# Attention, dense FFN and routed experts on one core: in the opening, key and query evictions split between ScalarE and VectorE, tile scores ordered ahead of weight work, and the global value rows copied on the chip

## The chip, the core and the metric

The kernel runs on one core of a Trainium2 chip. TensorE (PE) does matmuls and transposes, VectorE (DVE), ScalarE (ACT) and GpSimd (POOL) work elementwise, SyncE (SP) here only issues DMAs. Each engine takes its own instructions strictly in the order in which they were written, and a semaphore holds an instruction back until its inputs are there. The metric is the device time of one execution in microseconds (us), lower is better.

## What is computed

Local and global attention for 4 batches, 8 heads, 512 local and 32 global positions, head width 64; its output goes through a dense FFN, and that through a routed FFN with 8 experts. Cut to what matters here:

```python
s_ll = scale * q_l @ k_l.T            # only keys within 32 positions; the rest is masked
s_lg = scale * q_l @ k_g.T
a_l  = softmax(concat([s_lg, s_ll]))  # per row: minus the maximum, exp, divided by the sum
out_l = a_l @ concat([v_g, v_l])
x = relu(x @ w_in) ** 2 @ w_out       # 512 -> 2048 -> 512, weights given as 64-bit floats
x = x + gate * (relu(x @ w1[e]) @ w2[e])   # rows with skip score > 0, one of 8 experts each
```

## The kernel before

**Tiles.** A tile is 128 query positions; two tiles are a block, 4 tiles a batch. Names carry the tile: `sc2_0` and `sc2_1` are the two halves (even and odd heads) of the scores of tile 2, `sm` the masked scores, `mx` their row maxima, `pT` the transposed probabilities, `po` the product with the values, `xt` its division by the row sums, `xtr` the transposed result, which ACT copies into `x0` for tiles 0 and 1. A tile goes through `attention(t)` in six steps: the scores of both halves with mask, maximum and exp of half 0; the same for half 1; two transposes of the probabilities with an eviction each; values and division; transpose of the result.

**Keys and queries of batch 0.** Heads lie apart in memory, so `load_k` and `load_q` bring them in as they lie and a copy (`puts`, tokens P00, P01, P0, P1) puts them into the order that the transposes want. `prep_k(b, p)` transposes one of four head pairs into PSUM and evicts it to `kT`; `prep_q(j)` does two pairs with two evictions each into `qT`. Their PSUM tiles (`ktr`, `qtr`, and also `sc*_1`, `ptr`, `xtr`) share two places, taken in turn, so every transpose waits for the eviction of the one before the last.

**Values.** A tile reads up to four windows of 96 local value rows, with the 32 global rows below them in partitions 96 to 127. `load_v` brings each window by one DMA and the global rows by another (192 KB and 64 KB); for tiles 0 and 1 into seven opening places, later into six rotating ones (`vr`), which get their global rows once per batch.

**Weights.** The dense weights come as 64-bit floats in 32 chunks of 128x512: for each quarter of the FFN four chunks `in_k` and four chunks `out_f`. Each chunk is rebuilt as a 32-bit float by ACT (L219, `rebase`) and three DVE instructions (L223, L227, L233). Token A does one step of that: L219 for chunk i+1, then L227 of i, L223 of i+1, L233 of i. L227 of a chunk waits for its L219. Block 0 uses the chunks of the first three quarters as they are, in 4-pass float matmuls.

**Dense FFN of block 0.** For f = 0 to 15: `first(f)` (four matmuls into `h`, relu on ACT into `g`), square (`gh`, on ACT after token E, on DVE after F), and one step later `second(f)` (four matmuls into `acc`).

**What sets the order.** SEQ is a list of tokens written out by hand: W fetches a weight chunk, A is the step above, V loads half of a tile's windows, `0a` is the next step of tile 0 of block 0, `0b` of tile 1, `1a`, `1b` of tiles 2 and 3, F0, E0, I0, H0 move the FFN of block 0. Every token writes its instructions to all engines at once, so a token's place in SEQ is its place on each engine. The line that the change of evictions rests on is, in `prep_k`:

```python
nc.scalar.copy(kT[b][:, p, 0:SL].rearrange("p (q j) -> p j q", j=TPB), tr)
```

Of the kernel before, what the change touches and what calls it, by code (L numbers as in the profile page):

```python
# [18 lines left out]


SEQ = """
    Lk01 Lk00 P00 Lg0 0G P01 Lq0 P0 00 02 V Lq1 01 0q W 03 W A W W 0a A V V 0a A W W A 0a 0b 0a 0b A 0b W P1 W 0a A
    0b A V 0a W 0b V A 1q W W A 0b V 1a W W F0 A W E0 1a W W A W V 1a A F0 W 1a I0 A 1b L9 1a H0 V A A W V E0 W 1a
    X0 H0 A A E0 H0 W H0 A H0 W 1b E0 Lg1 A A W W A E0 1b W H0 A 1b E0 A H0 A E0 Lv00 A W W W 1g A I0 C 1b A 1g I0 W
    A D H0 Lv01 1g W E0 A E0 A I0 1g W C C 1g C W E0 A 1g Lq2 C Lk10 A H0 1g I0 2q A C C F0 2G Lk11 E0 I0 20 C E0 21
    22 F0 1b F1 23 C D F0 H1 C C V R00 2a F1 D H1 E1 2a E1 D R00 2a H1 R00 R01 C H1 C C F1 I1 R01 V 2b R01 E1 D A F1
# [28 lines left out]
def attention_ffn_routed_experts(  # L55
# [22 lines left out]
    nc = tc.nc  # L78
    B, H, SL, D = q_l.shape
    SG = q_g.shape[2]  # L80
    P = 128
# [8 lines left out]
    TPB = SL // P  # L90
# [3 lines left out]
    WIN = 3 * SEG  # L94
# [176 lines left out]
    kT, kin, qT, qin, qgT, vgr = {}, {}, {}, {}, {}, {}  # L271
    xts, whole = {}, []
    puts = {}

    def heads(t):
        return t.rearrange("p (h d) -> p h d", h=H)
# [5 lines left out]
    def load_k(b, z):  # L282

        kin[b, z] = stage(f"k{b}_{z}").rearrange("p (j h d) -> p j h d", h=4, j=TPB)
        if b == 0:
            t = stage(f"k{b}_{z}_in").rearrange("p (h j d) -> p h j d", h=4, j=TPB)
            nc.sync.dma_start(t, k_l[b, 4 * z:4 * z + 4].rearrange("h (p j) d -> p h j d", j=TPB))  # L290
            puts[f"{b}{z}"] = lambda: nc.scalar.copy(kin[b, z], t.rearrange("p h j d -> p j h d"))
            return
        for h in range(4):
            nc.sync.dma_start(kin[b, z][:, :, h, :], k_l[b, 4 * z + h].rearrange("(p j) d -> p j d", j=TPB))
# [31 lines left out]
    def prep_k(b, p):  # L326
        tr = pair(f"ktr{b}_{p}")
        for j in range(TPB):
            two = kin[b, p // 2][:, j, 2 * (p % 2):2 * (p % 2) + 2, :]
            nc.tensor.transpose(tr[:, j, :], two.rearrange("p r d -> p (r d)"), ident)  # L330
        nc.scalar.copy(kT[b][:, p, 0:SL].rearrange("p (q j) -> p j q", j=TPB), tr)

    def prep_q(j):
        qT[j] = sb("qT", 1, [P, NPAIR, BLK], f"qT{j}")
        for z in range(2):
            tr = pair(f"qtr{j}_{z}").rearrange("p (a i) q -> p a i q", a=2)
            for a in range(2):
                for i in range(2):
                    h = 2 * (2 * z + a)
                    two = qin[j][:, i, h:h + 2, :]  # L340
                    nc.tensor.transpose(tr[:, a, i, :], two.rearrange("p r d -> p (r d)"), ident)
            for a in range(2):
                nc.scalar.copy(qT[j][:, 2 * z + a, :].rearrange("p (q i) -> p i q", i=2), tr[:, a])

    def window(tt, i):
        return min(max(tt * P + i * SEG - SEG, 0), SL - WIN)
# [6 lines left out]
    def load_v(t, part):  # L353
# [3 lines left out]
        for i in range(2 * part, 2 * part + 2):  # L357
# [4 lines left out]
            if t < 2:  # L362

                k, half = divmod(len(opening), 2)
                if half == 0:
                    opening_places.append(stage(f"v{k}"))
                w = opening_places[k][:, half * DM:(half + 1) * DM]
                opening.append(w)
                nc.sync.dma_start(heads(w[0:WIN]), v_l[b, :, w0:w0 + WIN, :].rearrange("h s d -> s h d"))
                nc.sync.dma_start(heads(w[WIN:P]), v_g[b].rearrange("h s d -> s h d"))  # L370
                vin[t, i] = w
                continue
            k = loaded[0] % 6
# [3 lines left out]
            nc.sync.dma_start(heads(windows[k][0:WIN]), v_l[b, :, w0:w0 + WIN, :].rearrange("h s d -> s h d"))  # L377
            if globals_in.get(k) != b:
                globals_in[k] = b
                nc.sync.dma_start(heads(windows[k][WIN:P]), v_g[b].rearrange("h s d -> s h d"))  # L380
            assert all(w is not windows[k] for w in vin.values())
            vin[t, i] = windows[k]

# [1195 lines left out]
```

## Time and profile before

| | |
|---|---|
| time, median of 3 runs | 712.71 us (711.06 to 715.13) |
| profiled execution | 706.99 us, span of the core 705.3 us |
| mean granted TensorE clock | 0.985 |
| busy in the span | PE 97%, DVE 56%, ACT 52%, POOL 23% |
| TensorE busy from 0 to 45 us | 31.8 us of 45 |
| DMA from 0 to 60 us | 16.18 MB, mean 270 GB/s |

Shares are means over the whole program. In the stretch that the change touches, roughly the first 50 us, they are others: TensorE has gaps and a granted clock of 0.5 to 1, and VectorE is the fullest engine. A granted clock of 1 is 2.4 GHz, 0.5 is 1.2 GHz.

### The profile page before, as it was taken

How to read it: one execution, taken by the hardware profiler on the slowest of the kernel's cores; microseconds unless marked ns; L12 is line 12 of the kernel's file. 1: busy time of each engine (PE TensorE's matmuls, PEld its weight loads, DVE VectorE, ACT ScalarE, POOL GpSimd, SP SyncE). 2: the span in 40 equal slices, each digit the busy share in tenths (PEclk: the TensorE clock that was granted, in tenths of full speed). 3: DMA queues.
4: the chain of work that ended last, by engine and by line, in shares of the span. 5: the costliest groups of instructions: out<-in, count | busy, mean ns of one | idle time of the engine just before them, and what ended most of it. 6: DMA issues, size and time to landing. Idle time of an engine off the chain costs nothing. (4 is left out here: it accounts for less than half of the span.)

```text
span 705.3 us, 18628 instructions
## 1 busy us (share of the span) xinstructions
PE 680.9 (97%) x7621; PEld 573.8 (81%) x7621; DVE 395.0 (56%) x1072; ACT 365.2 (52%) x939; POOL 163.9 (23%) x206
## 2 busy tenths in 40 slices
PE   6689998999999999999999999999999999999996
PEld 4566667889888988888888998888887887898875
DVE  1889964872655165275426526544238733915985
ACT  5767568675535555453465445344434514614863
POOL 6000053453212212211211221122220432401311
PEclk8799999999999999999999999999999999999998
DMA  9999643064063401306340120410026689952930
GB/s 276 247 303 288 235 117 80 2 161 96 2 147 90 111 32 36 84 2 147 99 102 32 45 67 2 162 62 1 32 87 194 213 268 346 372 218 82 359 123 22
DMA packets 118841, 94.20 MB, mean 134 GB/s; under 512 B 84805, under 2 KB 91973, under 8 KB 118740
## 3 DMA queue, kind: packets, MB, share of 16 engines
q1 hardware_dynamic: 108352, 71.01, 35.9%
q10 hardware_dynamic: 8292, 15.48, 6.8%
q0 software_dynamic: 2096, 6.36, 2.7%
q8 instruction: 64, 1.05, 0.6%
q14 instruction: 37, 0.30, 0.2%
HBM read 80.57 MB, written 12.66 MB: 132 GB/s over the span
## 5 line engine op out<-in xcount | busy, mean ns | idle before, releaser
L184 POOL TENSOR_TENSOR gl<-g,gh 128x256 fp32r<-128x256 f32 x107 | 79.5, 743 | 302.8 <-ACT gh L183 142.3
L700 PE MATMUL h<-xh,w_in 128*128 128x256 f32 x464 | 135.1, 291 | 0.7 <-ACT xh L183 0.7
L701 PE MATMUL h<-xl,w_in 128*128 128x256 f32 x464 | 129.7, 280 | 0.3 <-DVE xl L184 0.3
L702 PE MATMUL h<-xh,w_in 128*128 128x256 f32 x464 | 129.8, 280 | 0.0
L725 PE MATMUL acc<-w_out,gh 128*128 128x512 f32 x232 | 97.6, 421 | 1.5 <-ACT gh L183 1.5
L727 PE MATMUL acc<-w_out,gl 128*128 128x512 f32 x232 | 91.9, 396 | 0.2
L726 PE MATMUL acc<-w_out,gh 128*128 128x512 f32 x232 | 91.7, 395 | 0.0
L700 PEld LDWEIGHTS h<-xh,w_in 128*128 128x128 f32 x464 | 87.2, 188 | 4.2 <-ACT xh L183 0.9
L701 PEld LDWEIGHTS h<-xl,w_in 128*128 128x128 f32 x464 | 87.3, 188 | 2.6 <-DVE xl L184 0.5
L704 ACT ACTIVATE g<-h 128x256 f32<-128x256 f32 x128 | 48.7, 381 | 77.0 <-PE h L702 43.7
L702 PEld LDWEIGHTS h<-xh,w_in 128*128 128x128 f32 x464 | 87.2, 188 | 0.0
L433 ACT ACTIVATE sm<-sm,mx 128x128 f32<-128x128 f32 x120 | 46.7, 390 | 49.5 <-DVE mx L431 49.5
L741 DVE TENSOR_TENSOR g<-h,g 128x256 f32<-128x256 f32 x53 | 22.2, 419 | 85.5 <-ACT g L704 85.5
L183 ACT CAST gh<-g 128x256 fp32r<-128x256 f32 x116 | 47.1, 406 | 42.2 <-DVE g L741 40.1
L727 PEld LDWEIGHTS acc<-w_out,gl 128*128 128x128 f32 x232 | 43.6, 188 | 11.9 <-POOL gl L184 1.3
L725 PEld LDWEIGHTS acc<-w_out,gh 128*128 128x128 f32 x232 | 43.6, 188 | 8.5 <-ACT gh L183 1.9
L726 PEld LDWEIGHTS acc<-w_out,gh 128*128 128x128 f32 x232 | 43.8, 189 | 5.7
L426 DVE TENSOR_TENSOR sm<-sc,mask 128x512 f32<-128x512 f32 x30 | 20.6, 687 | 23.3 <-PE sc L413 22.6
L255 POOL TENSOR_TENSOR w_in<-st_raw_in,w_in 128x512 fp32r<-128x512 f32 x10 | 13.0, 1308 | 80.0 <-ACT w_in L251 80.0
L743 ACT ACTIVATE g<-g 128x256 f32<-128x256 f32 x63 | 26.3, 417 | 5.0 <-ACT g L704 2.5
L413 PEld LDWEIGHTS sc<-kT,qT 64*32 64x32 f32 x2048 | 25.2, 110 | 4.3 <-issue 3.5
L413 PE MATMUL sc<-kT,qT 64*32 64x32 f32 (+1 forms) x2048 | 27.4, 230 | 0.0
(718 smaller groups left out, 1461.9 us busy)
## 6 DMA issues: line engine op xcount, KB each, us to landing
st_e<-in_moe_w_dram SPq DMA_DIRECT2D x46, 512.0 KB, 7.5
vr<-in_v_l_dram SPq DMA_DIRECT2D x49, 192.0 KB, 4.3
st_raw_in<-in_moe_w_in_dram SPq DMA_DIRECT2D x16, 512.0 KB, 6.6
st_raw_out<-in_moe_w_out_dram SPq DMA_DIRECT2D x16, 512.0 KB, 8.2
st_e<-in_moe_w_dram ACTq DMA_DIRECT2D x12, 512.0 KB, 5.5
x2d<-x ACTq DMA_DIRECT2D x19, 256.5 KB, 3.7
st_gv<-in_v_l_dram SPq DMA_DIRECT2D x8, 512.0 KB, 4.5
out_dram<-x ACTq DMA_DIRECT2D x16, 256.0 KB, 3.5
```

The source lines that it names most:

```text
L183: nc.scalar.copy(hi, src)
L184: (lo_engine or nc.vector).tensor_tensor(out=lo, in0=src, in1=hi.bitcast(F32), op=ALU.subtract)
L413: nc.tensor.matmul(scs[g][SEG * i:SEG * (i + 1), p, cols], lhsT=q[rows, p, SEG * i:SEG * (i + 1)], rhs=kT[b][rows, p, keys], start=True, s ...
L433: nc.scalar.activation(sm[:, hh, :], sm[:, hh, :], AF.Exp, bias=mx[:, hh:hh + 1], scale=SCALE, accum_out=osum[:, 2 * hh + g:2 * hh + g + 1],)
L700: nc.tensor.matmul(h, lhsT=wh, rhs=xh[:, k, :], start=(k == 0), stop=False)
L701: nc.tensor.matmul(h, lhsT=wh, rhs=xl[:, k, :], start=False, stop=False)
L702: nc.tensor.matmul(h, lhsT=wl, rhs=xh[:, k, :], start=False, stop=(k == KD - 1))
L704: nc.scalar.activation(g, h, AF.Relu)
L725: nc.tensor.matmul(acc[z], lhsT=gh[:, c], rhs=wh, start=first_one, stop=False)
L726: nc.tensor.matmul(acc[z], lhsT=gh[:, c], rhs=wl, start=False, stop=False)
L727: nc.tensor.matmul(acc[z], lhsT=gl[:, c], rhs=wh, start=False, stop=last_one)
L743: nc.scalar.activation(square, g, AF.Square)
```

## The change

Three things, all in the opening.

1. Of the copies and evictions that ACT did for keys and queries, DVE takes the reordering copy of the second half of the keys (P01), the evictions of head pairs 2 and 3 in `prep_k`, and of the second pairs of the first query block in `prep_q`.
2. The first part of SEQ is rewritten. The two halves of a tile's scores follow each other (`0a 0a`, `0b 0b`) with the A tokens behind them, the first two weight chunks are fetched ahead of the values, the second block's queries are loaded later, and F0 stands ahead of `1a`. From token X0 on nothing differs; the set of instructions up to there is the same but for points 1 and 3.
3. The global value rows of batch 0 come by one DMA; POOL copies them from there to the other six opening places and to the six rotating ones. SP issues 12 DMAs of 64 KB less, and POOL runs 12 copies of 32x512 more.

```diff
@@ SEQ
-    Lk01 Lk00 P00 Lg0 0G P01 Lq0 P0 00 02 V Lq1 01 0q W 03 W A W W 0a A V V 0a A W W A 0a 0b 0a 0b A 0b W P1 W 0a A
-    0b A V 0a W 0b V A 1q W W A 0b V 1a W W F0 A W E0 1a W W A W V 1a A F0 W 1a I0 A 1b L9 1a H0 V A A W V E0 W 1a
+    Lk01 Lk00 P00 Lg0 0G P01 Lq0 P0 00 02 W W V 01 0q W W 03 A 0a V 0a A Lq1 0a 0a A V W 0b 0b V 0a W A W P1 0a 0b
+    0b W A W V 0b 0b W V 1q W F0 A 1a W A E0 A 1a A W V F0 A 1a W W I0 A 1a A 1b W W W L9 1a H0 V A A A W V E0 W 1a
@@ load_k
-            puts[f"{b}{z}"] = lambda: nc.scalar.copy(kin[b, z], t.rearrange("p h j d -> p j h d"))
+            copy = nc.vector.tensor_copy if z else nc.scalar.copy
+            puts[f"{b}{z}"] = lambda: copy(kin[b, z], t.rearrange("p h j d -> p j h d"))
@@ prep_k
-        nc.scalar.copy(kT[b][:, p, 0:SL].rearrange("p (q j) -> p j q", j=TPB), tr)
+        copy = nc.vector.tensor_copy if b == 0 and p > 1 else nc.scalar.copy
+        copy(kT[b][:, p, 0:SL].rearrange("p (q j) -> p j q", j=TPB), tr)
@@ prep_q
-                nc.scalar.copy(qT[j][:, 2 * z + a, :].rearrange("p (q i) -> p i q", i=2), tr[:, a])
+                copy = nc.vector.tensor_copy if j == 0 and z else nc.scalar.copy
+                copy(qT[j][:, 2 * z + a, :].rearrange("p (q i) -> p i q", i=2), tr[:, a])
@@ load_v, the seven opening places
+                if len(opening) == 1:
+                    nc.sync.dma_start(heads(w[WIN:P]), v_g[b].rearrange("h s d -> s h d"))
+                else:
+                    nc.gpsimd.tensor_copy(w[WIN:P], opening[0][WIN:P])
                 nc.sync.dma_start(heads(w[0:WIN]), v_l[b, :, w0:w0 + WIN, :].rearrange("h s d -> s h d"))
-                nc.sync.dma_start(heads(w[WIN:P]), v_g[b].rearrange("h s d -> s h d"))
@@ load_v, the six rotating places
-                nc.sync.dma_start(heads(windows[k][WIN:P]), v_g[b].rearrange("h s d -> s h d"))
+                if b == 0:
+                    nc.gpsimd.tensor_copy(windows[k][WIN:P], opening[-1][WIN:P])
+                else:
+                    nc.sync.dma_start(heads(windows[k][WIN:P]), v_g[b].rearrange("h s d -> s h d"))
```

VectorE ahead of tile 0's scores and in them, before (a chunk's three instructions are those on `st_raw`):

```order
L310 COPY st_q0_213<-st_q0_in_214 128x1024
L223 TENSOR_SCALAR st_raw_in_0_0_256<-st_raw_in_0_0_256 128x512
L426 TENSOR_TENSOR sm0_0_339<-sc0_0_273,mask0_75 128x512
L430 TENSOR_REDUCE mx0_0_341<-sm0_0_339 128x4
L431 TENSOR_SCALAR mx0_0_341<-mx0_0_341 128x4
L227 SCALAR_TENSOR_TENSOR st_raw_in_0_0_256<-st_raw_in_0_0_256 128x512
L223 TENSOR_SCALAR st_raw_in_1_0_264<-st_raw_in_1_0_264 128x512
L233 SCALAR_TENSOR_TENSOR st_raw_in_0_0_256<-st_raw_in_0_0_256 128x512
L426 TENSOR_TENSOR sm0_1_362<-sc0_1_274,mask0_75 128x512
```

The same place after:

```order
L292 COPY st_k0_1_188<-st_k0_1_in_189 128x1024
L311 COPY st_q0_213<-st_q0_in_214 128x1024
L333 COPY kT0_198<-ktr0_2_223 128x4x128
L346 COPY qT0_242<-qtr0_1_250 128x2x128 x2
L333 COPY kT0_198<-ktr0_3_261 128x4x128
L223 TENSOR_SCALAR st_raw_in_0_0_229<-st_raw_in_0_0_229 128x512
L435 TENSOR_TENSOR sm0_0_336<-sc0_0_270,mask0_75 128x512
L439 TENSOR_REDUCE mx0_0_338<-sm0_0_336 128x4
L440 TENSOR_SCALAR mx0_0_338<-mx0_0_338 128x4
L435 TENSOR_TENSOR sm0_1_350<-sc0_1_271,mask0_75 128x512
```

One key copy, two key evictions and two query evictions have come to DVE, that of `ktr0_2` behind the query copy, and the second half of the scores follows the first at once; between tile 1's halves no chunk stood before or stands now.

VectorE from the division of tile 1 (`xt1`) to the scores of tile 2, before:

```order
L461 TENSOR_TENSOR xt1_598<-po1_563,osum1_390 128x512
L227 SCALAR_TENSOR_TENSOR st_raw_out_2_492<-st_raw_out_2_492 128x512
L223 TENSOR_SCALAR st_raw_out_3_495<-st_raw_out_3_495 128x512
L233 SCALAR_TENSOR_TENSOR st_raw_out_2_492<-st_raw_out_2_492 128x512
L227 SCALAR_TENSOR_TENSOR st_raw_out_3_495<-st_raw_out_3_495 128x512
L223 TENSOR_SCALAR st_raw_in_0_1_561<-st_raw_in_0_1_561 128x512
L233 SCALAR_TENSOR_TENSOR st_raw_out_3_495<-st_raw_out_3_495 128x512
L426 TENSOR_TENSOR sm2_0_714<-sc2_0_648,mask1_101 128x512
```

and after:

```order
L470 TENSOR_TENSOR xt1_596<-po1_561,osum1_391 128x512
L227 SCALAR_TENSOR_TENSOR st_raw_out_0_389<-st_raw_out_0_389 128x512
L223 TENSOR_SCALAR st_raw_out_1_517<-st_raw_out_1_517 128x512
L233 SCALAR_TENSOR_TENSOR st_raw_out_0_389<-st_raw_out_0_389 128x512
L435 TENSOR_TENSOR sm2_0_709<-sc2_0_643,mask1_101 128x512
L439 TENSOR_REDUCE mx2_0_711<-sm2_0_709 128x4
L440 TENSOR_SCALAR mx2_0_711<-mx2_0_711 128x4
```

At `xt1` the chunk in hand is `out_0` where it was `out_2`, and one step of weight work stands between `xt1` and tile 2's scores where there were two. On TensorE, behind the transposes of the second query block, the four matmuls of `h0_0` now stand ahead of the 128 of `sc2`; before, `sc2` came first.

ScalarE from the result of tile 1 to the eviction of tile 2's transposed probabilities, before (L704 is the relu, L743 the square of an FFN step):

```order
L468 COPY st_x0_559<-xtr1_633 128x4x128
L433 ACTIVATE sm2_0_714,osum2_647<-sm2_0_714,mx2_0_716 128x128 x4
L704 ACTIVATE g0_0_732<-h0_0_727 128x256
L219 ACTIVATE st_raw_in_1_1_625<-st_raw_in_1_1_625 128x512
L743 ACTIVATE gh0_0_740<-g0_0_732 128x256
L704 ACTIVATE g0_1_747<-h0_1_742 128x256
L433 ACTIVATE sm2_1_749,osum2_647<-sm2_1_749,mx2_1_751 128x128 x4
L219 ACTIVATE st_raw_in_2_1_627<-st_raw_in_2_1_627 128x512
L444 COPY pT2_0_779<-ptr2_0_774 128x512
```

and after:

```order
L477 COPY st_x0_531<-xtr1_598 128x4x128
L346 COPY qT1_614<-qtr1_0_615 128x2x128 x2
L346 COPY qT1_614<-qtr1_1_622 128x2x128 x2
L713 ACTIVATE g0_0_636<-h0_0_631 128x256
L219 ACTIVATE st_raw_out_1_517<-st_raw_out_1_517 128x512
L442 ACTIVATE sm2_0_709,osum2_642<-sm2_0_709,mx2_0_711 128x128 x4
L219 ACTIVATE st_raw_out_2_523<-st_raw_out_2_523 128x512
L752 ACTIVATE gh0_0_724<-g0_0_636 128x256
L713 ACTIVATE g0_1_731<-h0_1_726 128x256
L219 ACTIVATE st_raw_out_3_547<-st_raw_out_3_547 128x512
L442 ACTIVATE sm2_1_737,osum2_642<-sm2_1_737,mx2_1_739 128x128 x4
```

The relu of the first FFN step has moved ahead of tile 2's exps, its square still stands behind them and behind one more weight step; two weight steps follow the second half's exps before `pT2_0`, where one did.

## Rows read from the trace of the kernel before

**Rows 1.** The page: busy us, share of the span, instructions.
```profile
PE 680.9 (97%) x7621; PEld 573.8 (81%) x7621; DVE 395.0 (56%) x1072; ACT 365.2 (52%) x939; POOL 163.9 (23%) x206
```
**Rows 2.** Windows: stretch, length, busy PE, PEld, DVE, ACT, POOL; granted clock, DMA, GB/s.
```profile
16.57:69.85 53.28, 44.66 (x716) 32.52 (x717) 48.14 (x97) 36.36 (x113) 0.00 (x0) 0.90 1.05 277
```
**Rows 3.** Timeline, 0 to 45 us and DVE at 82: start, length; keys and queries.
```profile
8.05 1.06 ACT L291 COPY st_k<-st_k_in 128x1024 f32<-128x1024 f32 x1
9.26 0.69 DVE L310 COPY st_q<-st_q_in 128x1024 f32<-128x1024 f32 x1 [7.87 <-DMA st_q_in<-in_q_l_dram]
...
10.31 2.08 ACT L331 COPY kT<-ktr 128x512 f32<-128x512 f32 x2 [0.20 <-PE ktr L330]
...
11.44 2.12 PE L341 MATMUL qtr<-ident,st_q 128*128 128x128 f32 x8 [0.16 <-ACT kT L331]
...
14.36 2.04 PE L413 MATMUL sc<-kT,qT 64*32 64x96 f32 x128
...
82.20 0.67 DVE L507 COPY gpT<-gptr 128x512 f32<-128x512 f32 x1
```
**Rows 4.** Timeline, 0 to 45 us: scores, exps, weight steps and division, tiles 0, 1.
```profile
16.57 0.69 DVE L426 TENSOR_TENSOR sm<-sc,mask 128x512 f32<-128x512 f32 x1 [2.73 <-PE sc L413]
...
18.09 0.68 DVE L227 SCALAR_TENSOR_TENSOR st_raw_in<-st_raw_in 128x512 int32<-128x512 int32 x1
18.22 0.40 ACT L433 ACTIVATE sm<-sm,mx 128x128 f32<-128x128 f32 x1 [2.19 <-DVE mx L431]
...
19.64 0.68 DVE L426 TENSOR_TENSOR sm<-sc,mask 128x512 f32<-128x512 f32 x1
...
22.83 1.22 ACT L219 ACTIVATE st_raw_in<-st_raw_in 128x512 f32<-128x512 f32 x2
...
25.06 0.68 DVE L426 TENSOR_TENSOR st_sm<-sc,mask 128x512 f32<-128x512 f32 x1
...
28.25 0.56 ACT L444 COPY pT<-ptr 128x512 f32<-128x512 f32 x1
...
35.03 0.69 DVE L461 TENSOR_TENSOR xt<-po,osum 128x512 f32<-128x512 f32 x1
```
**Rows 5.** Windows of 1 us, columns as in rows 2: TensorE idle, then busy again.
```profile
24.00:25.00 1.00, 0.00 (x0) 0.00 (x0) 1.00 (x3) 0.52 (x2) 0.00 (x0) 1.00 0.98 365
...
26.00:27.00 1.00, 0.00 (x0) 0.00 (x0) 0.97 (x3) 0.30 (x1) 0.00 (x0) 0.50 1.04 426
...
32.00:33.00 1.00, 1.00 (x19) 0.65 (x21) 1.00 (x4) 1.00 (x3) 0.00 (x0) 0.64 0.87 308
```
**Rows 6.** Timeline, 33 to 130 us: scores of tile 2 and the first FFN steps.
```profile
36.42 1.62 PE L413 MATMUL sc<-kT,qT 64*32 64x96 f32 x128
36.53 0.59 ACT L468 COPY st_x<-xtr 128x512 f32<-128x512 f32 x1
...
37.98 3.51 PE L697 MATMUL h<-st_x,st_raw_in 128*128 128x256 f32 x15
...
38.71 0.68 DVE L426 TENSOR_TENSOR sm<-sc,mask 128x512 f32<-128x512 f32 x1
...
42.72 0.40 ACT L743 ACTIVATE gh<-g 128x256 f32<-128x256 f32 x1
...
42.99 0.49 PE L697 MATMUL h<-st_x,st_raw_in 128*128 128x256 f32 x1 [1.50 <-issue]
...
49.64 1.27 PE L451 MATMUL po<-vr,pT 128*32 128x64 f32 x64
...
58.44 1.96 PE L723 MATMUL acc<-st_raw_out,gh 128*128 128x512 f32 x4
```
**Rows 7.** Timeline, 76 to 130 us: a GpSimd instruction and a VectorE one beside it.
```profile
82.60 1.30 POOL L255 TENSOR_TENSOR w_in<-st_raw_in,w_in 128x512 fp32r<-128x512 f32 x1 [69.10 <-ACT w_in L251]
...
83.32 1.13 DVE L227 SCALAR_TENSOR_TENSOR st_raw_in<-st_raw_in 128x512 int32<-128x512 int32 x1
```
**Rows 8.** Waits from 0 to 130 us: us in total, times, longest.
```profile
DVE st_raw_in L223 <- DMA st_raw_in<-in_moe_w_in_dram: 3.5, 1, 3.5
```

## The prediction
> **What bounds the kernel now.** The page first: TensorE is busy for 97% of the span [rows 1], so over the whole program its work is the bound, and a change that removes none of that work can only win where TensorE stands idle or runs at the low clock. Then the opening by windows: between the first scores and 69.85 us VectorE is busy for 48.14 of 53.28 us, TensorE for 44.66 [rows 2]. Both are near full there, and VectorE is the fuller one; what it has to do up to that point is the same set of instructions before and after. So the question is not which engine gets less work, but whether the new order leaves VectorE or TensorE waiting longer for the other. I read the timeline for that: when TensorE starts tile 2's scores (36.42) and the first FFN step (37.98), and when it reaches `second(3)` of block 0 at 58.44 [rows 6], the first point behind which TensorE is fed without gaps. From token X0 on the order is the same, so a shift of TensorE at 58.44 is carried to the end, unless a later wait adds to it.
>
> **Step 1, evictions on VectorE.** ACT loses a key copy of 1.06 us, two key evictions of about 1.04 and a pair of query evictions [rows 3]. Little of it counts. VectorE may not evict `ktr0_2` before its query copy, which waits for the DMA until 9.26 and takes 0.69; the eviction ends at about 10.65. Meanwhile TensorE needs about 1.0 us for four transposes (eight took 2.12 [rows 3]), and it has `ktr1`, both `qtr` and `ktr3` to do behind ACT's eviction of `ktr0_0` at about 9.9: through the two shared PSUM places I get `ktr1` to 10.9, ACT's eviction to 12.0, `qtr1` to 13.05, `ktr3` to 14.0, scores from 14.0 to 16.2. Before it was 14.36 to 16.40 [rows 3]. The gain is 0.2 us. What a VectorE eviction with a stride of four costs no row shows; its bounds are 0.67, a plain one of that size, and 1.04, ACT's of the same form [rows 3]. I take 0.67, since it is the same engine; at 1.04 `ktr3` would still be evicted by 15.1, ahead of the fourth head pair of the scores at 15.8, so it changes nothing.
>
> **Step 2, both halves first.** A half costs VectorE 1.52 us (16.57 to 18.09), a weight step 1.55 (18.09 to 19.64), four exps 1.56, a rebase on ACT 0.61 [rows 4]. Before, tile 1's mask started at 25.06 [rows 4]. Now: halves of tile 0 from 16.37 to 19.4; exps from 18.0 to 21.2; the rebase of chunk 1 behind them to 21.8, for which VectorE's second weight step waits 0.9 us; that step ends at 23.4, and tile 1 starts there, 1.65 us earlier. From this start to the division `xt1` it took 9.97 us, to 35.03 [rows 4]. Now: 4.75 to the end of all exps, 0.61 rebase, then the copy of tile 0's result and two evictions (0.59, 0.56, 0.56 [rows 4, 6]) with the last transposes between them, then the values. That is 8.0 us at 2.4 GHz and, with transposes and values at half speed, 9.1 at 1.2. The trace shows TensorE idle at 24 to 27 and its granted clock at 0.50 from 26, back only after some 5 us of work, at 32.6 [rows 5]. After the change TensorE idles from about 24.7, when the values of tile 0 are done, to `xt0` at 28.0, so I take 1.2 GHz: `xt1` at 32.5, 2.5 us earlier, and the full clock from about 33.
>
> **Step 3, what that is worth.** From `xt1` to the end of the `x0` copy it is 2.1 us (35.03 to 36.53 and 0.59), and 0.5 more for the last query transposes: `h0_0` starts at 35.1 instead of 37.98. But `sc2`, 1.6 us, was ahead of it and is now behind: with 1.75 for `h0_0` (15 of 16 matmul records of two steps take 3.51), the scores of tile 2 end at D = 35.1 + 1.75 + 1.6 = 38.4. Before it was 37.98 [rows 6]. So 2.9 us earlier for the FFN is 0.4 us later for tile 2.
>
> **Step 4, what waits for D.** VectorE, done with `xt1` at 33.1, has one weight step, to 34.7, and then waits for `sc2` until 38.55: 3.9 us of idle on the engine that had 5.1 in all over 53 us [rows 2]. Before, it filled this stretch with two steps and started tile 2 at 38.71 [rows 6]; the steps now come behind. On ACT the square of step 0 stands behind tile 2's exps and a rebase: mask D+0.15, exps D+1.8 to D+3.35, rebase to D+3.95, square 0.40 [rows 6] to D+4.35. TensorE has finished `h0_1` at D+1.75 and waits for that square 2.65 us, to D+4.4. VectorE's second half of tile 2 follows two weight steps, of which the second waits for that rebase: it ends at D+7.0, its exps at D+8.75, and two rebases and `pT2_0` follow to D+10.5. `sc3` needs the PSUM place that `pT2_0` frees, so it starts at D+10.5, 1.5 us after TensorE could. Then `sc3` 1.65, values 1.2, `acc1` 1.9, `h0_3` 1.75, the next `xtr` 0.45: D+17.4. The square of step 2 stands behind tile 3's exps (D+17.7) and that of step 3 behind three rebases and two copies (D+21.8), so `second(3)` starts at D+21.9 = 60.3, where it was 58.44 [rows 6]. That is 1.9 us later. The break-even is D = 36.5.
>
> **Step 5, behind that.** VectorE reaches chunk 19 at about D+34.5 = 72.9; block 0's step 8 wants it at 73.6, so 0.7 us is left. Later TensorE wants the evicted probabilities of the global attention on VectorE, whose copy of 0.67 started at 82.20 [rows 3], just ahead of need; with VectorE 2.8 us late and TensorE 1.9, this may add 0 to 0.8. I take 0.4.
>
> **Step 6, global values by POOL.** No transfer is waited for in the opening after the first: VectorE's one wait for weights is 3.5 us, at 13.4 [rows 8], ahead of the scores. So 12 issues less are costed at nothing; what hides them is VectorE's backlog of chunks. POOL's 12 copies run from about 12 to 22 us, when it has nothing else to do but the second query copy, which has 10 us to spare. SP waits for no copy. A VectorE step beside a POOL instruction took 1.13 us instead of 0.68 [rows 7], so each overlap may cost 0.45; most copies fall ahead of the scores or into VectorE's 0.9 us wait for the rebase, so I take 0 and keep 0 to 1.8 (four overlaps, those with the weight steps of tile 0). The Trainium skill, page "SBUF — State Buffer", section "SBUF: two separate sides", speaks against this part of the change: GpSimd and VectorE share one pair of SBUF ports by an exclusive lock, and whoever comes second is blocked for a whole instruction when VectorE reads two SBUF inputs. The row with 1.13 us agrees. By that rule every copy that meets a weight step would cost, and the sum would be up to 1.8 higher.
>
> **The sum.** 1.9 + 0.4 = 2.3 us more. The profiled execution of 706.99 (span 705.3) would come to 709.3; the median of the runs shown lies 5.7 above it, and 712.71 + 2.3 = 715.0. I forecast 715.0. A measurement of this kernel can tell about 0.5% from no change, which is 3.6 us, 709.1 to 716.3, so this counts as no change.
>
> **Rivals.** *The clock falls again (slower).* The place is TensorE's new wait of 2.65 us ahead of `second(0)`. For it speaks that rows 5 show 0.50 after an idle stretch of that kind; against it, that this stretch was longer, with not one matmul in the windows at 24 and 26 us. It decides if the granted clock is 0.5 for 4 us or more between 40 and 50 us. Behind the wait stand `second(0)`, four transposes and `h0_2`, some 4.1 us of work, which would take twice as long; 1.6 us of that falls into the waits of step 4. Price 2.5: 717.5. *The gain stays.* If VectorE's backlog has more room than I give it, and the full clock holds through tile 1, TensorE keeps what `h0_0` gains: `xt1` at 31.4, `h0_0` at 34.0, and if the squares and `pT2_0` are not late, 2.4 for the start (4.0 less the 1.6 of `sc2`) and the stall of 1.50 at 42.99 [rows 6], which need not come again: 3.9 less, 708.8. Against it: the order of ACT, which puts the square behind exps that wait for `sc2`. *The transfers are the bound.* The DMA engines are full in this stretch (a share of 1.05 [rows 2]); 12 transfers of 64 KB are 0.79 MB, at 277 GB/s 2.8 us. If that came off the path: 709.9. Against it, the missing waits [rows 8]. *POOL blocks VectorE:* plus 1.8, 716.8.
>
> **How the numbers follow.** Forecast 0.45, the clock 0.25, the gain 0.18, POOL 0.07, transfers 0.05. Walking four engines by hand is good to about 2 us, so the forecast gives 0.40 to within 0.5% and 0.05 to slower; the clock 0.20 slower, 0.05 within; the gain, which lies near the bound, 0.13 faster, 0.05 within; POOL 0.05 slower, 0.02 within; transfers 0.05 faster. That makes faster 0.18, within 0.5% 0.52, slower 0.30. The range reaches from just under the gain to above the clock with half of POOL's price: 708.0 to 719.0.
>
> **What would show it.** Right: `h0_0` at 34 to 36 us, the scores of tile 2 ending at 37.4 or later, VectorE idle for 3 to 4 us ahead of them, TensorE waiting for ACT's square ahead of `second(0)`, and `second(3)` 1 to 3 us behind 58.44. Step 1 is wrong if the first scores end before 15.5. Wrong as a whole if `second(3)` starts before 58 us, or if a shift there is gone by 130 us.

## The result, and the profile after

The changed kernel is slower: 715.95 us median of 13 runs (714.47 to 721.04), the kernel before 710.31 (708.5 to 715.13) beside it, ratio 1.0084, 95% interval [1.0069, 1.0100]. That is 4.9 to 7.1 us more. The predicted 715.0 and its range hold the time, but the likeliest case, no change within 0.5%, did not come: the loss was put at 2.3 us and is 5.6.

The first profiled execution of the changed kernel took 721.04 us, its slowest. The rows here are from a second one, 715.65 us (span 713.9); the run is named changed_again. Its page, busy us, share of the span and instructions:

```profile
PE 684.6 (96%) x7621; PEld 575.6 (81%) x7621; DVE 401.0 (56%) x1077; ACT 362.2 (51%) x934; POOL 172.8 (24%) x218
```

TensorE does the same 7621 instructions as in [rows 1]. The timeline of TensorE through the opening (start, length, instruction, count, idle time ahead of it):

```profile
13.95 2.14 PE L422 MATMUL sc<-kT,qT 64*32 64x96 f32 x128
...
21.56 2.37 PE L422 MATMUL sc<-kT,qT 64*32 64x96 f32 x128
23.86 1.49 PE L460 MATMUL po<-st_v,pT 128*32 128x64 f32 x44
29.01 0.85 PE L460 MATMUL po<-st_v,pT 128*32 128x64 f32 x20 [3.65 <-issue]
30.66 1.11 PE L280 MATMUL xtr<-ident,xt 128*128 128x128 f32 x4 [0.79 <-DVE xt L470]
31.56 2.00 PE L451 MATMUL ptr<-ident,st_sm 128*128 128x128 f32 x8
33.49 2.26 PE L460 MATMUL po<-st_v,pT 128*32 128x64 f32 x64
...
38.36 1.90 PE L706 MATMUL h<-st_x,st_raw_in 128*128 128x256 f32 x8
40.19 1.62 PE L422 MATMUL sc<-kT,qT 64*32 64x96 f32 x128
...
46.13 3.63 PE L732 MATMUL acc<-st_raw_out,gh 128*128 128x512 f32 x4 [2.39 <-ACT gh L752]
...
52.30 1.64 PE L422 MATMUL sc<-kT,qT 64*32 64x96 f32 x128
...
63.27 2.06 PE L732 MATMUL acc<-st_raw_out,gh 128*128 128x512 f32 x4
```

Tile 2's scores end at D = 41.81 (40.19 + 1.62), where the prediction had 38.4 and the trace of before 38.04 [rows 6]. The last row is `second(3)`, at 63.27 where it was 58.44 [rows 6]: 4.8 us of the loss stand there. In the middle of tile 0's values, after 44 of 64 matmul records, TensorE stops for 3.65 us for nothing that the profile shows. VectorE in the same stretch:

```profile
14.05 1.11 DVE L333 COPY kT<-ktr 128x512 f32<-128x512 f32 x1
...
16.25 0.69 DVE L435 TENSOR_TENSOR sm<-sc,mask 128x512 f32<-128x512 f32 x1 [0.47 <-POOL st_v L375]
...
20.23 1.53 DVE L233 SCALAR_TENSOR_TENSOR st_raw_in<-st_raw_in 128x512 int32<-128x512 int32 x1
21.71 1.07 DVE L227 SCALAR_TENSOR_TENSOR st_raw_in<-st_raw_in 128x512 int32<-128x512 int32 x1
22.70 0.84 DVE L223 TENSOR_SCALAR st_raw_in<-st_raw_in 128x512 int32<-128x512 int32 x1
23.46 1.09 DVE L233 SCALAR_TENSOR_TENSOR st_raw_in<-st_raw_in 128x512 int32<-128x512 int32 x1
24.47 0.68 DVE L435 TENSOR_TENSOR st_sm<-sc,mask 128x512 f32<-128x512 f32 x1
...
29.91 0.69 DVE L470 TENSOR_TENSOR xt<-po,osum 128x512 f32<-128x512 f32 x1 [1.91 <-PE po L460]
...
35.79 0.69 DVE L470 TENSOR_TENSOR xt<-po,osum 128x512 f32<-128x512 f32 x1 [1.79 <-PE po L460]
...
41.91 0.69 DVE L435 TENSOR_TENSOR sm<-sc,mask 128x512 f32<-128x512 f32 x1 [3.88 <-PE sc L422]
```

These are the rows that answer to [rows 4]: tile 1's mask at 24.47 (25.06 before), its division `xt1` at 35.79 (35.03). VectorE was free for tile 0's division at 28.0 and waited 1.91 us for the stopped values. Behind it stand 3.88 us of idle time ahead of tile 2's mask.

Further on, the wait of TensorE for a square at 121.37 us before (0.73 us) comes at 127.16, 5.8 us later. And in the expert stage TensorE waits 1.58 us for an eviction where the run without GpSimd copies, below, waits 0.17; changed_again first, then that run:

```profile
603.91 0.41 PE L1183 MATMUL ertr_rest_a<-ident,er_rest_a 128*128 128x128 f32 x2 [1.58 <-DVE eg_rest_a L1185]
```
```profile
600.44 0.41 PE L1177 MATMUL ertr_rest_a<-ident,er_rest_a 128*128 128x128 f32 x2 [0.17 <-DVE eg_rest_a L1179]
```

The profiled executions of before and of changed_again differ by 8.7 us, more than the medians, because that of before is a quick one, 3.3 us under its median here.

### The profile page after: what moved, and what is told of

The parts are those of the page before. It is cut to its first block, busy times and chain, and to the rows that moved or that the text cites. A ratio compares the mean times of both kernels' runs of the same rounds, so it can differ in the third digit from the quotient of the medians.

```text
span 719.3 us, 18638 instructions
## 1 busy us (share of the span) xinstructions
PE 687.5 (96%) x7621; PEld 579.2 (81%) x7621; DVE 400.9 (56%) x1077; ACT 361.5 (50%) x934; POOL 172.2 (24%) x218
## 5 line engine op out<-in xcount | busy, mean ns | idle before, releaser
L732 PE MATMUL acc<-st_raw_out,gh 128*128 128x512 f32 x48 | 25.6, 657 | 3.9 <-ACT st_raw_out L219 3.9
L752 ACT ACTIVATE g<-g 128x256 f32<-128x256 f32 x63 | 26.2, 416 | 5.1 <-ACT g L713 2.6
```

The source lines that it names most:

```text
L752: nc.scalar.activation(square, g, AF.Square)
```

## The experiments

**Theory A** is the prediction's: the order makes tile 2's scores late, and VectorE, ScalarE and TensorE wait in turn. **Theory B** came from the profile after: TensorE runs out of instructions, and the new order lets it run without the pauses that hid this. **Theory C** puts the loss on the evictions and the GpSimd copies. Each ratio is to runs of the kernel before on the same chip. D and `second(3)` are from the one profiled execution of each; "late" is the wait in the expert stage just shown. The times are medians of 5 to 12 runs (11 to 27 of before).

| run | median us | ratio to before, 95% | D | second(3) | late |
|---|---|---|---|---|---|
| before | 709.35 to 710.31 | 1 | 38.04 | 58.44 | 0.2 |
| changed_again | 715.86 | 1.0079 [1.0053, 1.0105] | 41.81 | 63.27 | 1.6 |
| order_alone | 712.66 | 1.0048 [1.0029, 1.0067] | 40.48 | 61.91 | 0.2 |
| old_order | 709.49 | 1.0003 [0.9988, 1.0019] | 38.91 | 58.73 | 0.2 |
| no_gpsimd_copies | 711.90 | 1.0033 [1.0018, 1.0049] | 39.79 | 61.18 | 0.2 |
| scores_first | 712.60 | 1.0037 [1.0020, 1.0054] | 39.01 | 60.74 | 1.4 |
| copies_for_nothing | 715.64 | 1.0088 [1.0073, 1.0102] | 41.03 | 62.47 | 1.6 |
| stream_moved | 726.22 | 1.0239 [1.0212, 1.0266] | 39.25 | 61.39 | 0.2 |
| stream_moved_and_back | 717.30 | 1.0103 [1.0080, 1.0125] | 43.32 | 65.80 | 1.6 |
| before_stream_moved | 711.17 | 1.0021 [1.0008, 1.0034] | 39.56 | 59.34 | 1.4 |
| idle_filled_no_copies | 713.90 | 1.0070 [1.0045, 1.0095] | 39.94 | 61.37 | 1.4 |
| idle_filled_changed | 717.18 | 1.0105 [1.0087, 1.0122] | 42.68 | 65.49 | 1.7 |
| idle_filled_before | 713.19 | 1.0048 [1.0032, 1.0064] | 44.25 | 63.47 | 1.4 |

The last three columns hang on one execution each, and that is a weak hold. In the first profiled execution of the changed kernel D is 43.32, `second(3)` 66.78 and the late wait 1.7. stream_moved and stream_moved_and_back are the same program up to the end of the opening, and there D differs by 4.1 us and `second(3)` by 4.4. So what a part costs is read from the times; the columns show where it may lie.

The second run of the changed kernel, and what was expected of it:

> The changed kernel itself once more, since the one profiled run of it lies 5 us above its median. Theories A (the order makes tile 2's scores late) and B (TensorE also runs out of instructions): 5 to 6 us slower than before; in the profile the stop of 3 to 4 us after 349 matmul records is there again; under B the second stop, after 600 records, is there too, and second(3) starts at 63 us or later; under A alone second(0) starts 4.4 us behind the end of tile 2's scores and second(3) at 61 to 62.5 us.

The time and the stop are as expected; a second stop ahead of `second(0)` is not there (the first profiled execution started `second(0)` 1.6 us after its square was done, 2.4 us behind a packet of the instruction queue, as explained below), and `second(3)` is at 63.27, late enough for theory B without its second stop.

### Which part of the change costs

order_alone is the kernel before with the two new lines of `SEQ`, nothing else.

> The kernel before with the new token order of the opening and nothing else; evictions stay on ScalarE, all global values come by DMA. Theory A (the order makes tile 2's scores late, as the prediction had it): VectorE idles 3 to 4 us ahead of tile 2's mask and TensorE waits ahead of second(0); 2 to 4 us slower than before. Theory B (TensorE also runs out of instructions, because the new order lets tile 1's scores and tile 0's values run without a pause): a stop of about 4 us that the trace puts down to issue, after some 349 matmul records, and 4 to 6 us slower than before, nearly all of what the changed kernel loses. Theory C (the loss comes from the evictions on VectorE and the copies on GpSimd): within 1.5 us of before.

old_order is the changed kernel with the two old lines.

> The changed kernel with the token order of before: evictions shared with VectorE and global values copied by GpSimd, and nothing else. Theories A and B: within 1.5 us of before, and TensorE's only long stop for issue is the one of 1.5 us near 43 us. Theory C: 3 us or more slower than before.

no_gpsimd_copies takes part 3 out of the changed kernel:

```diff
-                if len(opening) == 1:
-                    nc.sync.dma_start(heads(w[WIN:P]), v_g[b].rearrange("h s d -> s h d"))
-                else:
-                    nc.gpsimd.tensor_copy(w[WIN:P], opening[0][WIN:P])
                 nc.sync.dma_start(heads(w[0:WIN]), v_l[b, :, w0:w0 + WIN, :].rearrange("h s d -> s h d"))
+                nc.sync.dma_start(heads(w[WIN:P]), v_g[b].rearrange("h s d -> s h d"))
...
-                if b == 0:
-                    nc.gpsimd.tensor_copy(windows[k][WIN:P], opening[-1][WIN:P])
-                else:
-                    nc.sync.dma_start(heads(windows[k][WIN:P]), v_g[b].rearrange("h s d -> s h d"))
+                nc.sync.dma_start(heads(windows[k][WIN:P]), v_g[b].rearrange("h s d -> s h d"))
```

> The changed kernel with the twelve global values brought by DMA as before, so the new order and the evictions on VectorE stay. Theories A and B: within 1 us of the changed kernel (VectorE's weight steps near 22 to 25 us get faster by up to 2 us, but tile 1's scores end no earlier). Theory C: 2 us or more faster than the changed kernel.

The order alone costs 3.4 us (0.48% of 709), evictions and copies in the old order nothing (0.2, interval -0.9 to 1.3), the changed kernel without the copies 2.3. So no theory stands alone: the copies cost 0.46 to 0.51%, some 3.3 to 3.6 us, on top of the new order, and in the old one copies and evictions together cost nothing. What the copies cost there by themselves no run shows, since the evictions may give some of it back. In the old order the copies lie at 12.8 to 22.1 us; a weight step beside them is slower there too (1.11, 0.84, 1.09), D is 0.9 us later than before, and `second(3)` 0.3. The gain of the evictions, 712.66 to 711.90, lies within the intervals.

order_alone shows theory A's chain without the copies, and theory B's stop too:

```profile
23.97 0.86 PE L451 MATMUL po<-st_v,pT 128*32 128x64 f32 x43
27.89 0.86 PE L451 MATMUL po<-st_v,pT 128*32 128x64 f32 x21 [3.06 <-issue]
...
38.86 1.62 PE L413 MATMUL sc<-kT,qT 64*32 64x96 f32 x128
...
44.77 2.07 PE L723 MATMUL acc<-st_raw_out,gh 128*128 128x512 f32 x4 [2.36 <-ACT gh L743]
...
61.91 2.07 PE L723 MATMUL acc<-st_raw_out,gh 128*128 128x512 f32 x4
```

The stop is after 43 records here (44 in the changed kernel), 3.06 us long. Tile 2's scores end at 40.48, and `second(0)` starts 4.3 us behind them, `second(3)` 21.4. The same places in no_gpsimd_copies:

```profile
28.05 0.53 PE L454 MATMUL po<-st_v,pT 128*32 128x64 f32 x20 [2.50 <-issue]
...
38.17 1.62 PE L416 MATMUL sc<-kT,qT 64*32 64x96 f32 x128
...
44.08 2.07 PE L726 MATMUL acc<-st_raw_out,gh 128*128 128x512 f32 x4 [2.36 <-ACT gh L746]
...
61.18 2.06 PE L726 MATMUL acc<-st_raw_out,gh 128*128 128x512 f32 x4
```

### The copies, or the missing transfers?

copies_for_nothing is no_gpsimd_copies with the twelve copies beside the transfers, written to a buffer that nothing reads until it is filled much later:

```diff
+    scratch = xgT.rearrange("p k c -> p (k c)")
...
+                if len(opening) > 1:
+                    nc.gpsimd.tensor_copy(scratch[WIN:P], opening[0][WIN:P])
...
+                if b == 0:
+                    nc.gpsimd.tensor_copy(scratch[WIN:P], opening[-1][WIN:P])
```

> The run without GpSimd copies (all global values by DMA), and beside it the twelve copies of the changed kernel on GpSimd at their places, written to a place that nothing reads. It tells what makes the changed kernel some 3.5 us slower than the run without the copies. Theory C1 (the copies: they block VectorE, or hold back what TensorE waits for): 2.5 us or more slower than the run without them, 5 to 6 us slower than before, the stop of TensorE after 349 records 3.5 us or longer. Theory C2 (the twelve missing DMA issues let the weights' transfers be issued sooner, and the pieces of the instruction stream queue behind them): within 1 us of the run without the copies, the stop 2.5 to 3.2 us.

The time is C1's, 3.7 us over the run without them (3.9 by the ratios); so twelve copies cost that much even with all transfers in place, and no cost of the missing transfers is left to explain. The way is not the one that C1 named: the stop is 2.16 us. The second six copies run here from 28.94 to 34.06 us, because their source comes late, and VectorE's steps between the two divisions beside them take longer:

```profile
28.97 1.12 DVE L234 SCALAR_TENSOR_TENSOR st_raw_in<-st_raw_in 128x512 int32<-128x512 int32 x1
30.02 1.10 DVE L228 SCALAR_TENSOR_TENSOR st_raw_in<-st_raw_in 128x512 int32<-128x512 int32 x1
31.04 0.85 DVE L224 TENSOR_SCALAR st_raw_out<-st_raw_out 128x512 int32<-128x512 int32 x1
31.80 1.11 DVE L234 SCALAR_TENSOR_TENSOR st_raw_in<-st_raw_in 128x512 int32<-128x512 int32 x1
```
```profile
34.50 0.74 PE L281 MATMUL xtr<-ident,xt 128*128 128x128 f32 x4 [2.02 <-DVE xt L469]
35.04 2.00 PE L344 MATMUL qtr<-ident,st_q 128*128 128x128 f32 x8
36.83 2.65 PE L705 MATMUL h<-st_x,st_raw_in 128*128 128x256 f32 x8
```

Four instructions take 4.18 us where the same four take 2.49 without a copy beside them (0.69, 0.69, 0.42, 0.69). TensorE waits 2.02 us for `xt1`, and its granted clock, 1.00 at 32 to 34 us, is 0.74 and then 0.50 in the next two windows of 2 us: `h0_0` takes 2.65 us and not 1.90. In the changed kernel GpSimd's query copy and the last six copies lie at 20.0 to 26.1 us, beside the weight steps that end at 24.47 (1.53, 1.07, 0.84, 1.09 above); tile 1's mask is only 0.2 us later for it than without the copies (24.28), but the stop ends 1.0 us later (29.01 and 28.05) and tile 1's values run at half clock (2.26 us and 1.46). That the copies hold the stop is not shown: in copies_for_nothing it is short, and in scores_first, without a copy, it ends at 28.50. So the price of the copies is shown, and the way to it is seen in copies_for_nothing, where they run later; by which way they cost it in the changed kernel stays open.

### The place of FFN step 0

scores_first is no_gpsimd_copies with one token moved:

```diff
-1q W F0 A 1a W A E0 A 1a
+1q W A 1a F0 W A E0 A 1a
```

> The run without GpSimd copies (new order, evictions on VectorE), with one token moved: the first FFN step of block 0 behind tile 2's scores instead of ahead of them, as in the order before. Theory A: tile 2's scores end 1.8 us earlier, VectorE's idle time ahead of its mask falls from 3.88 to about 2.1 us, second(3) comes 1.5 to 1.8 us earlier and the kernel is 1.5 to 1.8 us faster than that run, within 1 us of before. Theory B alone (the loss is the stop after 349 records): within 0.7 us of that run.

D comes 0.8 us earlier, not 1.8, because the stop is 3.15 us in place of 2.50 and a second one of 0.42 falls into tile 2's scores. `second(3)` follows D by 21.7 us, as theory A says, 0.4 us earlier than without the move, and the late wait (1.4 in place of 0.2) takes that back. The time is that of no_gpsimd_copies, within the 0.7 us that was expected if theory B alone held; the 1.5 to 1.8 us of theory A did not come. So the place of FFN step 0 by itself does not carry the price of the order.

### Where TensorE stops

stream_moved puts 96 tiny matmuls behind the warm-up of the changed kernel, stream_moved_and_back 32 more at the end of `SEQ`'s work:

```diff
         warm(WARM)
+        o = ps.tile([P, DM], F32, tag="x2", bufs=2, name="pad")
+        for _ in range(96):
+            nc.tensor.matmul(o[0:32, 0:1], lhsT=idle[:, 0:32], rhs=idle[:, 0:1], start=True, stop=True)
...
+        o = pair("pad2").rearrange("p a k -> p (a k)")
+        for _ in range(32):
+            nc.tensor.matmul(o[0:32, 0:1], lhsT=ones[:, 0:32], rhs=ones[:, 0:1], start=True, stop=True)
```

> The changed kernel with 96 tiny matmuls (one column, 32 columns of weights) behind the warm-up, while TensorE waits for the first keys; the result of none is used. They do no work of the kernel, but move every later instruction of TensorE by 192 places in its stream. Theory B: the 256-instruction steps at which TensorE stood still (349 and 600 records) now fall elsewhere: the stop of 3.97 us in tile 0's values goes, tile 1's division comes at 33 to 34 us, not 37.3, the stop ahead of second(0) goes too unless it waits for the square, and the kernel is 3 to 5 us faster than the changed one, within 2 us of before. Theories A and C: both stops are put down to other work and stay where they are in the program; within 1 us of the changed kernel.

> The changed kernel with the 96 tiny matmuls at the start, and 32 more behind the opening and the first two FFN blocks, so that from there on the stream's 256-instruction steps fall within one instruction of where the changed kernel has them. The two stops in the expert stage that stream_moved showed (4.4 and 2.4 us) should be gone, and the time shows what the stops of the opening alone cost. Theory B: 3 to 5 us faster than the changed kernel, 0.5 to 2.5 us slower than before. Theory A: the stops were slack ahead of VectorE, and the time is within 1.5 us of the changed kernel. If the two expert stops stay, they have another cause than the steps.

In stream_moved the stop in tile 0's values is gone, and others have come, two of them in the expert stage (waits of TensorE in all, times, longest; then its timeline):

```profile
PE ewh_a L948 <- issue: 4.4, 1, 4.4
PE eh_rest_a L1172 <- issue: 2.4, 1, 2.4
```
```profile
24.21 1.45 PE L460 MATMUL po<-st_v,pT 128*32 128x64 f32 x64
28.84 1.11 PE L280 MATMUL xtr<-ident,xt 128*128 128x128 f32 x4 [3.18 <-DVE xt L470]
```

Moving the stream moves the stops: that half of theory B holds, and with the steps moved back both expert stops are gone. The other half, that the kernel gets faster, fails in both times. In the profile of stream_moved the opening itself is quicker than in changed_again, by 2.6 us at D and 1.9 at `second(3)`, and the two expert stops (6.8 us) take back more than that. In stream_moved_and_back the same opening is slower by 1.5 and 2.5, so one profile of each can't say what the stop is worth. Without the stop TensorE waits 3.18 us for `xt0` instead; and the tiny matmuls delayed the first scores (16.09 us in stream_moved_and_back, 13.95 without).

before_stream_moved is the kernel before with 118 and 10 of them:

> The kernel before with 118 tiny matmuls at the start and 10 behind the opening and the first two FFN blocks (256 instructions in all), for the one stop of 1.50 us at 42.99 us. Theory B: that stop goes, a smaller one may come in tile 3's scores, and the kernel is 0 to 1.5 us faster than before. Theory A says nothing of it; without a part of the stream in it, the stop stays between the 15th and the 16th record of the first two FFN steps, and the time is that of before.

The stop of 1.50 us is gone and no other is long enough to be listed, yet the kernel is 1.3 us slower (0.6 to 2.4): the first scores start at 15.78 (14.36 [rows 3]), `second(3)` is 0.9 us later, and the late wait is there.

The last three put them where TensorE waits anyway, so that the first scores aren't touched: behind tile 0's scores and ahead of `second(0)` in the two new-order kernels, and in the kernel before behind tile 0's scores, behind the first transposes of its second half, and 10 at the end of `SEQ`'s work (Z is a token that emits so many; the first pair of lines is the new order's, the second that of before):

```diff
-03 A 0a V 0a ... E0 A 1a A W V F0
+03 A 0a Z64 V 0a ... E0 A 1a Z64 A W V F0
-W W 0a A V V 0a ... 0a 0b 0a 0b A 0b
+W W 0a Z64 A V V 0a ... 0a 0b 0a Z54 0b A 0b
```

> The run without GpSimd copies with 64 tiny matmuls behind tile 0's scores and 64 ahead of second(0), both in stretches in which TensorE waits for ScalarE by 2.37 us; no result is used. The first 64 move the stream by 128 instructions, so that the step at 349 records falls into tile 1's scores and its piece is asked for some 5 us earlier; the second 64 move it back by one whole step. Unlike the matmuls at the start they cannot delay the first scores. Theory B: the stop of 2.5 to 3.1 us falls under 1 us, tile 0's division starts when VectorE is free (27.7 us, not 28.6), and the kernel is 0.5 to 2 us faster than without them. Theory A (the order and VectorE set the pace, the stop is slack): within 0.7 us. If the tiny matmuls keep the granted clock at 1.0 where it was 0.5 (18.7 to 24 us), tile 1's scores end up to 2 us earlier and that is seen apart.

> The changed kernel with the same 64 and 64 tiny matmuls. Theory B: the stop of 3.7 us falls to 1 us or less, tile 0's division starts near 28.0, tile 2's scores end at 38.5 to 39.5 us (41.8 without), second(3) at 60 to 61.5, and the kernel is 2 to 3.5 us faster than the changed one. Theory A: within 1 us of the changed kernel; tile 2's scores still end after 41 us.

> The kernel before with 64 tiny matmuls behind tile 0's scores, 54 behind the first transposes of its second half (TensorE waits 4.7 us there), and 10 behind the opening and the first two FFN blocks, 256 instructions in all: the stream stands as in before_stream_moved, but the first scores are not delayed. Theory B: the stop of 1.50 us at 42.99 us is gone and the kernel is 0.3 to 1.5 us faster than before, the fastest of all. If it is the tiny matmuls that cost in before_stream_moved (1.3 us), and not the later first scores, it is slower than before again.

All three are slower than without, by 2.6, 1.8 and 3.4 us (by the ratios), against theory B's price, and more than the 0.7 and 1 us that theory A allows. (In idle_filled_no_copies `second(3)` is only 0.2 us later than without; 1.2 us are the late wait.) But they show what the stops are. TensorE in idle_filled_before:

```profile
16.09 1.48 PE L1209 MATMUL pad<-ones 128*32 128x1 bf16 x53
21.27 0.46 PE L1209 MATMUL pad<-ones 128*32 128x1 bf16 x11 [3.70 <-issue]
...
22.70 2.26 PE L413 MATMUL sc<-kT,qT 64*32 64x96 f32 x113
26.65 0.29 PE L413 MATMUL sc<-kT,qT 64*32 64x32 f32 x15 [1.69 <-issue]
...
30.86 1.59 PE L451 MATMUL po<-st_v,pT 128*32 128x64 f32 x49
33.88 0.65 PE L451 MATMUL po<-st_v,pT 128*32 128x64 f32 x15 [1.43 <-issue]
...
40.67 0.43 PE L413 MATMUL sc<-kT,qT 64*32 64x96 f32 x25
42.41 1.84 PE L413 MATMUL sc<-kT,qT 64*32 64x32 f32 x103 [1.31 <-issue]
```

Count the matmul records ahead of each stop: 168 up to the first scores' end and 53 make 221; 11, 4 and 113 more make 349; then 475; then 599. The distances are 128, 126 and 124, whatever the work is, even in the middle of matmuls that wait for nobody. The long stop of the changed kernel is after record 348 (one less than here), and that of before [rows 6] after record 599. A matmul has a weight load of its own, so 126 records are some 252 instructions. At each stop a packet of the instruction queue arrives (64 of them with 1.05 MB in the kernel before, 16 KB each). In this kernel they are seen in the half microseconds from 18.5, 23.5, 31.0 and 39.5 us, and TensorE goes on 2.77, 3.15, 2.88 and 2.91 us after these marks. Over all fourteen profiles the 23 stops for issue behind the first scores end 2.2 to 3.0 us behind the start of a packet (in changed_again 26.58 and 29.01), the two in the expert stage of stream_moved among them (2.4 and 2.7). The packet of this row, from a window of 1 us (queue, packets, MB, share of the engines):

```profile
q8 instruction: 1, 0.02, 8.6%
```

The Trainium skill, page "Runtime: NRT & Kernel Launch", section "Instruction fetch mechanics", says that each engine is refilled in blocks of 16 KiB, 256 instructions, by a DMA queue of its own. The rows agree with that size. It calls the cost of a block's edge mostly hidden; in this opening, with the DMA engines' share at 1.05 [rows 2], the stops are 0.2 to 4.0 us long (4.0 in the first profiled execution of the changed kernel), where TensorE does a block's work before the next block is there.

## Why the prediction was right and wrong

- **Step 1, the evictions: right.** First scores from 13.95 to 16.1 (14.0 to 16.2 predicted). The strided eviction takes 1.11 us, a little above the upper bound of 1.04 and not the 0.67 chosen; as the step said of the bound, that changes nothing.
- **Step 2: right for VectorE, wrong for TensorE.** Tile 0's halves run from 16.25 to 19.3 (16.37 to 19.4 predicted), and VectorE is free for `xt0` at 28.0, as predicted to the tenth, but by luck: the mask of tile 1 came 1.1 us later than the 23.4 given, and from it to 28.0 it was 3.5 us and not 4.6. The failing term is the one that the working did not have: tile 0's values were taken as done at 24.7, and they stop until 29.01. `xt0` is 1.9 us late by that. From `xt0` to `xt1` it is 5.88 us, not 4.5: transposes of 1.11 and 2.00 us and values of 2.26 stand one behind another on TensorE, at 1.2 GHz (0.50 to 0.55 granted). `xt1` at 35.79, not 32.5.
- **Step 3: right in form.** From `xt1` to D it is 6.0 us (5.9 predicted). D is 41.8 for 38.4: 1.9 the stop, 1.4 the half-clock chain, 0.1 the rest. But the 1.8 that `h0_0` was to cost ahead of `sc2` did not come back in scores_first: 0.8 at D, 0.4 at `second(3)`, nothing in the time.
- **Step 4: right to a few tenths, counted from D.** VectorE idles 3.88 us (3.9), `second(0)` starts at D + 4.3 (D + 4.4), `sc3` at D + 10.5 (D + 10.5), `second(3)` at D + 21.5 (D + 21.9). In order_alone, no_gpsimd_copies, copies_for_nothing and changed_again `second(3)` is at D + 21.4 to 21.5 (D + 23.5 in the first profiled execution of the changed kernel); before it was D + 20.4. So the order loses 1.1 us behind D, and the rest through D. The predicted 1.9 is 4.8.
- **Step 5: a little small.** From 58.44 to the square at 121.37 us before, the changed kernel loses another 1.0, where 0.4 was taken and 0.8 was the bound. It is the same in order_alone and no_gpsimd_copies (0.9).
- **Step 6: wrong.** The copies were put at 0, with 1.8 as the bound; the runs give 3.3 to 3.9. In the profiles 2.1 of it stand at `second(3)` (63.27 and 61.18) and 1.4 in the late wait (1.6 and 0.2). The last six copies ran from 21.3 to 26.2 us, behind a query copy whose data came at 20.0, where the step had all of them done at about 22; four weight-step instructions beside these and the query copy took 4.53 us for 2.49, which alone is over the bound, and yet tile 1's mask was only 0.2 later than without them. The overlaps were judged by VectorE's spare time; that TensorE can fall to half clock behind a late VectorE (seen in copies_for_nothing), and that time can be lost 540 us later (if the late wait goes with the kernel, which is open), was in no term. On the Trainium skill's port lock ("SBUF — State Buffer", "SBUF: two separate sides") the trace agrees: weight-step instructions beside a copy took 1.07 to 1.53 us for 0.68. The twelve issues saved were worth nothing, as said.
- **The rival "the clock falls again"** came true in place and not in price: `second(0)` takes 3.63 us for 2.07, the clock is 0.51 from 46 to 48 us and at full again at 50, so low for some 3.5 us and not quite the 4 that it asked for. But `second(3)` is at D + 21.46 there and at D + 21.39 in no_gpsimd_copies, where the clock stays at 1.00 (windows of changed_again, then of that run; columns as in [rows 2]):

```profile
46.00:48.00 2.00, 1.87 (x2) 0.83 (x3) 2.00 (x4) 0.93 (x3) 0.00 (x0) 0.51 1.02 408
48.00:50.00 2.00, 2.00 (x7) 0.95 (x6) 1.93 (x6) 1.00 (x5) 0.00 (x0) 0.63 1.04 356
```
```profile
46.00:48.00 2.00, 2.00 (x13) 1.86 (x12) 1.94 (x5) 1.05 (x5) 0.00 (x0) 1.00 1.10 195
48.00:50.00 2.00, 1.26 (x8) 0.61 (x6) 1.59 (x4) 2.00 (x7) 0.00 (x0) 1.00 0.90 285
```

  All that it takes falls into the wait of `sc3` for `pT2_0`; the price of 2.5 was too high by 2.5.
- **"The gain stays"** listed the stop of 1.50 us at 42.99 as one that need not come again. It was the sign of what came instead: a stop for issue was in the rows, and its cause was not asked for.

Two of the prediction's own signs came out otherwise: `h0_0` starts at 38.36, not at 34 to 36, and `second(3)` is 4.8 us behind 58.44, not 1 to 3. The other signs are there.

So the time came out near the predicted one by luck: two terms of the sum were too small (D, the copies), and its base, the median of three runs, was 2.4 us above the median of 13. By the times the missing 3.3 us are the copies': without them the kernel is 2.3 us slower (1.3 to 3.5), the 2.3 of the sum, though D is 1.4 us later there than predicted.

**What stays open.** The stop's own price: it held VectorE for 1.9 us in the changed kernel, 1.2 in order_alone, 0.9 in no_gpsimd_copies, but every attempt to move it added instructions, and none was faster as a whole. Which of the order's moves carries its 3.4 us: only the place of FFN step 0 was tried by itself. By which way the copies cost their 3.3 to 3.9 us in the changed kernel. Why the packet comes at 26.5 us in the changed kernel and at 25.0 in order_alone and no_gpsimd_copies. And the late wait of 1.4 to 1.7 us, seen in eight of the twelve experiment profiles and not in those of before, old_order, order_alone, no_gpsimd_copies and stream_moved: ScalarE and VectorE go on there some 3 us after packets of the second instruction queue (599.5 and 600.0; 602.68 and 603.34), which looks like the same thing on those engines, but that is not shown. Both profiles of the changed kernel have it; with one profile of each other kernel, whether it goes with the kernel or with the execution isn't settled. No version beat the kernel before.

## What to carry over

Where an opening is full of small matmuls and the transfer engines are full too, count TensorE's instructions: running two groups back to back gains only what the supply of instructions allows, and a stop that the profile puts down to issue is to be looked up by its place in the stream before a gain is built on it. Price a GpSimd instruction beside a busy VectorE by rows, even if VectorE has room: here the copies cost 3.3 to 3.9 us where the steps beside them grew by some 2, and what hangs on VectorE next and TensorE's clock while it waits are the places to look. A chain counted from one point (here D) can be right to tenths while the point itself is off, so give most care to what sets that point. And take more than one profile before a difference of a few us at one place is believed: the same opening ran 4 us apart in two.

## What the runs showed of the hardware

- TensorE stops at fixed distances of 124 to 128 matmul records (some 250 instructions), and goes on 2.2 to 3.0 us behind the start of a packet of 16 KB on the instruction queue (23 stops in fourteen profiles); stops of 0.2 to 4.0 us in the opening, 2.4 and 4.4 in the expert stage of stream_moved. Tiny matmuls placed in TensorE's idle time were stopped in the same way, for 2.2 to 3.8 us in their own midst, and the transposes behind them came late by it.
- A VectorE instruction with one input, the int32 TENSOR_SCALAR of 128x512, takes 0.84 us beside a GpSimd copy (1.26 and 1.27 beside the query copy in no_gpsimd_copies and stream_moved_and_back) and 0.42 alone; so it is not only the ones with two inputs.
- An eviction from PSUM on VectorE with a stride of four, 128x512 f32, takes 1.08 to 1.15 us, a plain one 0.67 [rows 3]; ScalarE's of the same form 1.04 [rows 3] to 1.11.
